# Third expert's gathers after its predecessor's weights, the fallback as one loop, and two weight splits one step later

## The chip, the core and the metric

The kernel runs on one NeuronCore of a Trainium2 chip. The time is device microseconds (us) of one execution, the median over several executions. Engines are named as in the profile: PE (TensorE, matrix multiply; PEld its weight load), DVE (VectorE), ACT (ScalarE), POOL (GpSimd), SP (SyncE, which here only issues DMAs). [...]

## The reference

Three layers in a row: a linear attention with decay, a mixture of 8 experts in which every token takes the expert of its largest logit, and a mixture of 4 experts in which every token takes all four, weighted. 3072 tokens, 256 wide, hidden width 1024, all in float32.

```python
def _moe_ref(x, w_gate, w1, w2):                # 8 experts, one per token
    logits = x @ w_gate
    expert_idx = np.argmax(logits, axis=1)
    ...
    for e in range(E):
        mask = expert_idx == e
        xe = x[mask]
        h = np.maximum(xe @ w1[e], 0.0)
        out[mask] = gate_w[mask, None] * (h @ w2[e])

def _moe2_ref(x, domain_probs, w1, w2):         # 4 experts, all of them for each token
    p = domain_probs / (domain_probs.sum(-1, keepdims=True) + 1e-09)
    for e in range(E):
        h = np.maximum(x @ w1[e], 0.0)
        out += p[:, e:e + 1] * (h @ w2[e])

def reference(**kwargs):
    x = _attn_ref(...)                           # (4, 8, 768, 32), laid out as 3072 x 256
    return _moe2_ref(x=_moe_ref(x=x, ...), ...)
```

## The kernel before, in words

Every float32 matrix product is made of three matmuls on split operands: a value is cast to a rounded high part (`hi`, on ACT) and the rest is a low part (`lo`, a subtraction on DVE or POOL); the three are hi x hi, hi x lo, lo x hi. So each weight tile has a cast and a subtraction before PE can use it.

The program has three stages on the time line of the profiled execution. From 0 to about 113 us the attention runs and each group of tokens is routed. From 113 to 288 us the eight experts of the first mixture run, in an order of turns found at run time (the fullest first). From 292 us on the second mixture runs with the order of all its instructions written out by hand.

**Experts.** For each expert `e` the loop calls `gemm1x` (eight products `f` of 6 matmuls into PSUM tile `ph`, which has 3 buffers; ACT writes `hh`, DVE writes `hl`), `make_x(e + 1)` (PE transposes the next expert's token rows `xg`, tile `tpx`) and `gemm2x` (two products of 24 matmuls into `po`). Expert 0 is done in two halves of 256 and 216 columns. `gather_turn(e)` issues up to four indirect DMAs on POOL that fetch the token rows `xg` of turn `e`; `xg` has 8 buffers. `prep` splits the next expert's weights: the subtractions of the first weight matrix (`wl`, line 152) are on POOL, those of the second (line 150) on DVE. After each product `f` a `hook` takes one entry of a list `queue`: first the computation of each expert's first slot, then that of each token's place (`pl`, `place`, `t`, `ot`, six tiles `om`, a matmul `ip`), written to DRAM as `idd`, then 24 `fetch` gathers on POOL (line 1002) which bring each token's weights for the second mixture (`pgs`). The scheduler of the language orders instructions of this stage on each engine; `issue_after` holds one back behind another.

**Fallback.** If an expert has more tokens than its columns, `tc.If(left > 0)` (line 1043) runs eight loops of plain matmuls, one for each expert. With the inputs timed here `left` is 0: the profile holds no instruction of its lines 1044 to 1083, only the branch around them. In PE's program 509 instructions of the fallback stand between the branch and the second mixture, in DVE's 243.

**Second mixture.** A step is one `hidden` (seven products of 3 matmuls each into the PSUM banks x, z, w, y, lines 1113 to 1148) and one `output` (36 matmuls into `po`, line 1174) of the step before; 64 steps, four weight pairs `i` = 0 to 3 for each of four parts of the tokens and four experts. In a step ACT copies banks x, z, w to `s`, POOL adds `g`, DVE makes `u` and `c`, ACT and DVE make the high and low parts `h`. `split_pair` casts a pair's two weight tiles on ACT (lines 178, 180) and subtracts on POOL (179, 181); `sums_pair` makes four sums on POOL (172). For the first expert pairs 0 and 1 are split before the stage; pairs 2 and 3 are split at the end of the first two steps.

Of the kernel before, what the change touches and what calls it, by code (L numbers as in the profile page):

```python
# [8 lines left out]
F32 = mybir.dt.float32  # L9
# [10 lines left out]
P = 128  # L20
# [15 lines left out]
NSL = 512  # L36
NC = E1 * NSL // P + 1
BIG = 3 << 29
OUTSIDE = 16384


def body(tc, I, out):
    nc = tc.nc
    with ExitStack() as outer:
# [5 lines left out]
        xs = dp.tile([NT, D], F32, name="xs")  # L50
        pgd = dp.tile([NT, E2], F32, name="pgd")
        idd = dp.tile([NT + P, 1], I32, name="idd")
        zero = cp.tile([P, 1], I32, name="zero")
        nc.vector.memset(zero, 0)

# [813 lines left out]
        with ExitStack() as ctx:  # L869
# [88 lines left out]
            def gather_turn(e):  # L958
                gather(e, range(tiles(e)), xs, idr.rearrange("p e c -> p (e c)"), 4 * (e - STAY))
# [52 lines left out]
            for e in range(E1):  # L1012
                if e == E1 - 2:
                    operands = x_first()

                def hook(f, e=e):
                    if operands:
                        operands.pop(0)()
                    if queue and e and (e > 1 or len(queue) > NQ):
                        queue.pop(0)()  # L1020
                    if f % 4 == 3:
                        prep(e + 1, f // 4)
                    if e == 0 and f in (4, 6):
# [12 lines left out]
                if e == 0:  # L1036
                    gemm2x(0, hs, CAP0, CAPS[0], bass.ds(BASES[0], CAPS[0] - CAP0), lambda k: prep(1, 2 + k))
                else:
                    gemm2x(e, hs, 0, CAPS[e], bass.ds(BASES[e], CAPS[e]), lambda k: prep(e + 1, 2 + k))


            left = nc.values_load(tab[0:1, 3, 0:1], min_val=0, max_val=NT)
            with tc.If(left > 0, preferred_fallthrough_block=False), tc.tile_pool(name="fall", bufs=1) as fp:
                starts = nc.values_load_multi_w_load_instructions(tab[0:1, 1, :], min_val=0, max_val=NT)[1]
                turns = nc.values_load_multi_w_load_instructions(tab[0:1, 4, :], min_val=0, max_val=E1 - 1)[1]
                ends = nc.values_load_multi_w_load_instructions(tab[0:1, 2, :], min_val=0, max_val=NT)[1]
                for e in range(E1):
                    w1, w2 = (I[k][bass.ds(turns[e], 1)].rearrange("o r c -> (o r) c") for k in ("w1", "w2"))
                    with tc.For_i(starts[e], ends[e], P) as ws:
                        ix = fp.tile([P, 1], I32, name="ixf")  # L1050
                        nc.sync.dma_start(ix, idd[bass.ds(ws, P)])
                        xg = m1.tile([P, D], F32, tag="xg", name="xgf", bufs=8)
                        nc.gpsimd.indirect_dma_start(xg, None, xs, bass.IndirectOffsetOnAxis(ap=ix, axis=0))
                        xT = m1.tile([P, 2, P], F32, tag="xg", name="xTf", bufs=8)
                        tp = pm.tile([P, 2, P], F32, tag="oneC", name="tpf", bufs=2)
                        for k in range(2):
                            nc.tensor.transpose(tp[:, k, :], xg[:, k * P:k * P + P], ident)
                        nc.scalar.copy(xT, tp)
                        hf = fp.tile([P, NF, P], F32, tag="hf", name="hf")
                        for j in range(2):  # L1060
                            raw = [mp.tile([P, 512], F32, tag="hh", name="raw0f", bufs=10) for _ in range(2)]
                            for k in range(2):
                                nc.sync.dma_start(raw[k], w1[k * P:k * P + P, j * 512:j * 512 + 512])
                            for f in range(4):
                                ph = pm.tile([P, P], F32, tag="three", name="phf", bufs=3)
                                for k in range(2):
                                    nc.tensor.matmul(ph, raw[k][:, f * P:f * P + P], xT[:, k, :],
                                                     start=(k == 0), stop=(k == 1))
                                nc.scalar.activation(hf[:, 4 * j + f, :], ph, AF.Relu)
                        raws = []  # L1070
                        for j in range(4):
                            raw = mp.tile([P, 2, D], F32, tag="hl", name="raw1f", bufs=10)
                            nc.sync.dma_start(
                                raw, w2.rearrange("(k p) d -> p k d", p=P)[:, j * 2:j * 2 + 2, :])
                            raws.append(raw)
                        for k in range(2):
                            po = pm.tile([P, P], F32, tag="two", name="pof", bufs=2)
                            for f in range(NF):
                                nc.tensor.matmul(po, raws[f // 2][:, f % 2, k * P:k * P + P], hf[:, f, :],
                                                 start=(f == 0), stop=(f == NF - 1))  # L1080
                            dst = bass.ds(ws, P)
                            (nc.vector.tensor_copy if k else nc.scalar.copy)(x2[k][:, dst], po)
                x_again()

        m1s.close()
# [125 lines left out]
        for e in range(E2):  # L1211
            g = E1 + e
            for t in range(NTP):
                tn = (t + 1) % NTP if (e, t) != (E2 - 1, NTP - 1) else None
                for i in range(4):
                    step = 4 * t + i

                    def weights(when, f):
                        for gn, at in ((g + 1, step), (g, step + 16)):
                            if E1 < gn < E1 + E2 and at in when:  # L1220
                                f(gn, when[at])

# [24 lines left out]
                    held = (*held, (i, HP)) if held else (g, t, (i, HP))  # L1247
# [37 lines left out]
```

## Time and profile before

| | |
|---|---|
| median of 3 runs | 824.31 us (822.92 to 825.62) |
| profiled execution, its own time | 822.34 us |
| its span, first to last instruction | 820.6 us |
| mean granted PE clock | 0.969 |
| PE busy | 773.1 us, 94% of the span |
| DVE, POOL, ACT busy | 580.1, 480.2, 406.2 us |

The profiled execution is 1.97 us under the median of the runs shown; 1.7 us of its time lie outside the span. An engine's busy time is a union of its instructions' times. In rows of the time line the bracket at the end is the idle time of that engine just before the row and what ended it; "issue" means that the profile shows nothing for which it waited, "remote" that a semaphore ended it whose sender was not found.

### The profile page before, as it was taken

What the parts mean: (1) busy time and instruction counts of PE and PEld (TensorE: products, weight loads), DVE (VectorE), ACT (ScalarE), POOL (GpSimd) and SP (SyncE); (2) the same over time, 40 slices, a digit from 0 to 9 for tenths busy, and PEclk for the clock granted to TensorE, in tenths of its full rate; (3) what the DMA queues carried; (4) which work ended last, traced back from release to release, by engine and by line L of the source; (5) the groups of instructions that cost most, each with busy time, mean ns of one, the idle gap of its engine ahead of it and who ended that gap; (6) DMA issues with size and microseconds to landing.
All of it is one profiled execution on the core that took longest, in us unless ns stands there. A gap on an engine that the chain in (4) does not pass through costs nothing.

```text
span 820.6 us, 16313 instructions
## 1 busy us (share of the span) xinstructions
PE 773.1 (94%) x6296; PEld 728.4 (89%) x6296; DVE 580.1 (71%) x1050; ACT 406.2 (49%) x858; POOL 480.2 (59%) x538
## 2 busy tenths in 40 slices
PE   8879987899999969999999999999999999999994
PEld 5556577789999969999999999999999999999994
DVE  8697882665445656776887777978767877778853
ACT  5533343434455445455555455565554655554540
POOL 5546645624588065356876355977435886465634
PEclk8998997999999979999999999999999999999998
DMA  8943225433843310000000000100000000000001
GB/s 220 226 124 97 64 42 178 151 109 104 122 124 118 91 30 26 2 1 27 26 27 27 1 2 1 52 27 26 2 2 1 26 27 1 1 27 28 26 27 52
DMA packets 41688, 46.41 MB, mean 57 GB/s; under 512 B 10432, under 2 KB 30656, under 8 KB 41600
## 3 DMA queue, kind: packets, MB, share of 16 engines
q1 hardware_dynamic: 37040, 37.09, 16.9%
q0 software_dynamic: 3360, 7.13, 2.9%
q8 instruction: 51, 0.84, 0.4%
q10 hardware_dynamic: 1200, 1.05, 0.4%
q14 instruction: 37, 0.30, 0.1%
HBM read 38.90 MB, written 6.35 MB: 55 GB/s over the span
## 4 chain that ended last, share of the span: by engine, by line
PE 60%; issue 1%; POOL 1%; ACT 1%; DVE 0%; POOLq 0%; ACTq 0%
PE po L1174 32%; PE x L1113 9%; PE z L1113 8%; PE w L1113 8%; PE y L1113 4%; POOL out L1194 1%; ACT s L1126 0%; ACT xc L802 0%; PE poA L1174 0%; POOLq L1281 0%; POOL g L1131 0%; ACT wh L178 0%; POOL gap L1199 0%; DVE h L1122 0%; DVE c L1148 0%
## 5 line engine op out<-in xcount | busy, mean ns | idle before, releaser
L1174 PE MATMUL po<-w,h 128*128 128x256 f32 x2280 | 281.4, 281 | 0.3 <-DVE h L1122 0.3
L1174 PEld LDWEIGHTS po<-w,h 128*128 128x128 f32 x2280 | 279.0, 189 | 0.5 <-DVE h L1122 0.5
L1119 ACT ACTIVATE h<-c 128x384 fp32r<-128x384 f32 x192 | 98.8, 525 | 150.2 <-DVE c L1148 84.8
L1122 DVE SCALAR_TENSOR_TENSOR h<-c,h 128x384 fp32r<-128x384 f32 x192 | 150.2, 791 | 11.3
L1131 POOL TENSOR_TENSOR g<-s,s 128x384 f32<-128x384 f32 x64 | 65.1, 1017 | 145.7 <-ACT s L1130 145.7
L1133 DVE TENSOR_TENSOR u<-y,s 128x384 f32<-128x384 f32 x64 | 35.5, 555 | 75.2 <-ACT s L1130 70.1
L1113 PE MATMUL x<-xc,wh 128*128 128x384 f32 x256 | 67.4, 345 | 7.5 <-issue 4.1
L803 POOL TENSOR_TENSOR xc<-x,xc 128x384 fp32r<-128x384 f32 x32 | 36.5, 1140 | 51.0 <-ACT xc L802 50.7
L1113 PE MATMUL w<-xc,wh 128*128 128x384 f32 x256 | 66.2, 340 | 0.0
L1113 PE MATMUL z<-xc,wh 128*128 128x384 f32 x256 | 66.1, 340 | 0.0
L838 ACT ACTIVATE hh<-ph 128x216 fp32r<-128x216 f32 (+8 forms) x68 | 33.5, 495 | 57.5 <-PE ph L248 38.4
L248 PE MATMUL ph<-xh,wh 128*128 128x488 f32 (+8 forms) x142 | 51.2, 361 | 10.0 <-DVE hl L840 7.7
L1148 DVE TENSOR_TENSOR c<-u,g 128x384 f32<-128x384 f32 x64 | 60.4, 944 | 0.0
L840 DVE SCALAR_TENSOR_TENSOR hl<-ph,hh 128x216 fp32r<-128x216 f32 (+8 forms) x68 | 37.5, 557 | 28.1 <-ACT hh L838 22.1
L1126 ACT COPY s<-x 128x384 f32<-128x384 f32 x64 | 30.7, 480 | 53.4 <-PE x L1113 53.4
L152 POOL TENSOR_TENSOR wl<-raw,wh 128x1024 fp32r<-128x1024 f32 (+1 forms) x22 | 39.6, 1800 | 26.8 <-ACT wh L146 25.0
L1122 DVE SCALAR_TENSOR_TENSOR h<-x,h 128x384 fp32r<-128x384 f32 x64 | 35.7, 558 | 24.8 <-ACT h L1119 24.5
L803 POOL TENSOR_TENSOR xc<-ts,xc 128x384 fp32r<-128x384 f32 x46 | 52.4, 1153 | 0.0
L1113 PEld LDWEIGHTS x<-xc,wh 128*128 128x128 f32 x256 | 42.6, 190 | 11.0 <-ACT s L1126 6.1
L501 POOL TENSOR_TENSOR Sm<-S,smask 128x256 f32<-128x256 f32 x44 | 31.3, 729 | 35.9 <-DVE S L491 29.1
L248 PE MATMUL ph<-xh,wl 128*128 128x488 f32 (+8 forms) x142 | 50.3, 354 | 0.3 <-POOL wl L152 0.3
L248 PE MATMUL ph<-xl,wh 128*128 128x488 f32 (+8 forms) x142 | 50.1, 353 | 0.0
(236 smaller groups left out, 1743.9 us busy)
## 6 DMA issues: line engine op xcount, KB each, us to landing
raw<-in_w SPq DMA_DIRECT2D x30, 512.0 KB
raw<-in_v SPq DMA_DIRECT2D x32, 256.0 KB
xs<-xo SPq DMA_DIRECT2D x24, 128.0 KB
xz<-in_xt SPq DMA_DIRECT2D x6, 384.0 KB
CT<-in_CT SPq DMA_DIRECT2D x7, 192.0 KB
BT<-in_BT SPq DMA_DIRECT2D x7, 192.0 KB
bt<-in_bt SPq DMA_DIRECT2D x3, 384.0 KB
ar<-in_ar SPq DMA_DIRECT2D x3, 384.0 KB
```

The source lines that it names most:

```text
L152: ins = nc.gpsimd.tensor_sub(lo[:, :, a:a + n], raw[:, :, a:a + n], hi[:, :, a:a + n].bitcast(F32))
L248: mm = nc.tensor.matmul(ph, w[:, k, fs], x[k], start=(i == 0), stop=(i == 5))
L803: eng.tensor_sub(o[:, 1], src, o[:, 0].bitcast(F32))
L838: i0 = nc.scalar.activation(hh, ph, AF.Relu)
L840: i1 = nc.vector.scalar_tensor_tensor(hl, ph, 0.0, hh.bitcast(F32), op0=ALU.max, op1=ALU.subtract)
L1113: nc.tensor.matmul(bank[to], w[:, a], x[:, r], start=(m == 0 and to not in seen), stop=(m == 2), skip_group_check=True)
L1119: sc.activation(HP[n][0], src, AF.Relu)
L1122: v.scalar_tensor_tensor(HP[n][1], src, 0.0, HP[n][0].bitcast(F32), op0=ALU.max, op1=ALU.subtract)
L1131: nc.gpsimd.tensor_add(g_, s5, s7)
L1133: v.tensor_add(u2, bank["y"], s1)
L1148: v.tensor_add(c22, u2, g_)
L1174: nc.tensor.matmul(two[h], x[:, ts], w2[:, w, j], start=(i, j, h * (len(hs) - 1), m) == (0, 0, 0, 0), stop=(i, j, m) == (3, 1, 2), skip_gr ...
```

## The change

Three edits.

1. In the expert stage `gather_turn(2)` moves from behind expert 0's second `gemm1x` to behind its `gemm2x`, held back until the second `wl` of expert 1 (`LOW[0]`). The hook takes entries of `queue` in every product from expert 1 on (before, only the four first ones in expert 1), so the places are computed one expert earlier, and empty entries thin the fetches to three in four products.
2. The fallback becomes one loop over a list of parts made on DVE inside the branch, and the hint that the untaken arm should follow the branch goes.
3. In the second mixture the splits of pairs 2 and 3 move from steps 0 and 1 to steps 1 and 2; the sums of pair 3 move from step 0 to step 1, behind the split of pair 2.

```diff
-            NQ = NU + NU // 4 + 6
...
-            queue += [lambda u=u: fetch(u) for u in range(NU)]
+            queue += [f for u in range(NU) for f in [lambda u=u: fetch(u)] + [lambda: None] * (u % 3 == 2)]
...
-                    if queue and e and (e > 1 or len(queue) > NQ):
+                    if queue and e:
                         queue.pop(0)()
...
-                if e + 2 < E1:
+                if 0 < e < E1 - 2:
                     gather_turn(e + 2)
...
                 if e == 0:
                     gemm2x(0, hs, CAP0, CAPS[0], bass.ds(BASES[0], CAPS[0] - CAP0), lambda k: prep(1, 2 + k))
+                    with tc.issue_after(LOW[0]):
+                        gather_turn(2)
...
-            with tc.If(left > 0, preferred_fallthrough_block=False), tc.tile_pool(name="fall", bufs=1) as fp:
-                starts = nc.values_load_multi_w_load_instructions(tab[0:1, 1, :], min_val=0, max_val=NT)[1]
...
-                for e in range(E1):
-                    w1, w2 = (I[k][bass.ds(turns[e], 1)].rearrange("o r c -> (o r) c") for k in ("w1", "w2"))
-                    with tc.For_i(starts[e], ends[e], P) as ws:
+            with tc.If(left > 0), tc.tile_pool(name="fall", bufs=1) as fp:
...
+                with tc.For_i(0, parts_, 1) as part:
+                    cell = fp.tile([1, 2], I32, name="cell")
+                    nc.sync.dma_start(cell, lid[bass.ds(part, 1)])
...
-                            if g == E1 and step < 2:
-                                if step == 0:
+                            if g == E1 and step in (1, 2):
+                                split_pair(g, step + 1)
+                                if step == 1:
                                     sums_pair(g, 3)
-                                split_pair(g, step + 2)
```

PE's order at the branch, before: the fallback's eight loops (rows of one are shown, `tpf` to `pof`) stand between the branch of line 1043 and the first product `x` of the second mixture.

```order
L859 MATMUL po<-hh,wl_7_1_3832 128x376
L1042 TENSOR_LOAD tab
L1043 COMPARE_AND_BRANCH
L1043 UNCONDITIONAL_BRANCH
L1044 TENSOR_LOAD tab
L1046 TENSOR_LOAD tab
L1049 COMPARE_AND_BRANCH
L1049 UNCONDITIONAL_BRANCH x2
```

The same place of PE's order now, whole up to the first product:

```order
L1047 COMPARE_AND_BRANCH
L1087 TENSOR_LOAD all__4053
L1088 COMPARE_AND_BRANCH
L1088 UNCONDITIONAL_BRANCH x2
L1326 BRANCH_PREFETCH_HINT
L1102 MATMUL tpf<-ident,xgf 128x128 x2
L1112 MATMUL phf<-xTf,raw0f 128x128 x16
L1124 MATMUL pof<-hf,raw1f 128x128 x16
L1088 REGISTER_ALU
L1088 COMPARE_AND_BRANCH
L1088 UNCONDITIONAL_BRANCH
L1047 UNCONDITIONAL_BRANCH x2
```

One loop stands there in place of eight: in PE's program 72 instructions now belong to the arm that is jumped over (before 509), in DVE's 69 (before 243). Before, the untaken arm stood right behind the branch and the loops after it, so the way to the second mixture crossed all of them; now the taken jump goes over the one loop.

POOL's order from the end of expert 0's first half, before. `xg` are the gathers (`idr`: the turns' rows), `wl` the weight subtractions of experts 1 and 2.

```order
L265 DMA xg<-xs,idx 128x256 x2
L265 DMA xg<-xs,idr 128x256 x8
L152 TENSOR_TENSOR wl_1_0_2423<-raw_1_0_2302,wh_1_0_2422 128x1024
L265 DMA xg<-xs,idr 128x256 x2
L152 TENSOR_TENSOR wl_1_1_2467<-raw_1_1_2304,wh_1_1_2466 128x1024
L265 DMA xg<-xs,idr 128x256 x2
L988 TENSOR_TENSOR pl<-oneh,base 128x192
L265 DMA xg<-xs,idr 128x256 x2
L152 TENSOR_TENSOR wl_2_0_2696<-raw_2_0_2693,wh_2_0_2695 128x1024
```

And now:

```order
L267 DMA xg<-xs,idx 128x256 x2
L267 DMA xg<-xs,idr 128x256 x4
L154 TENSOR_TENSOR wl_1_0_2424<-raw_1_0_2303,wh_1_0_2423 128x1024
L154 TENSOR_TENSOR wl_1_1_2468<-raw_1_1_2305,wh_1_1_2467 128x1024
L267 DMA xg<-xs,idr 128x256 x8
L990 TENSOR_TENSOR pl<-oneh,base 128x192
L267 DMA xg<-xs,idr 128x256 x2
L154 TENSOR_TENSOR wl_2_0_2697<-raw_2_0_2694,wh_2_0_2696 128x1024
```

The run of eight gathers in front of expert 1's first subtraction is now a run of four; a run of eight (those of the third and the fourth expert) stands behind its second one.

DVE's order in expert 2 (products of 456 columns), before. `ot` and `om` are operands of the places' matmul.

```order
L840 SCALAR_TENSOR_TENSOR hl<-ph,hh 128x456 x2
L227 TENSOR_SCALAR t<-place 128x24
L840 SCALAR_TENSOR_TENSOR hl<-ph,hh 128x456
L217 TENSOR_TENSOR ot<-iota_76,t 128x576
L218 TENSOR_TENSOR ot<-ot,tokc 128x576
L840 SCALAR_TENSOR_TENSOR hl<-ph,hh 128x456
L228 SCALAR_TENSOR_TENSOR m<-t,place 128x24
L840 SCALAR_TENSOR_TENSOR hl<-ph,hh 128x456
L213 TENSOR_TENSOR om<-iota_74,m 128x512
```

And now, from the first product of expert 2:

```order
L842 SCALAR_TENSOR_TENSOR hl<-ph,hh 128x456
L230 SCALAR_TENSOR_TENSOR m<-t,place 128x24
L842 SCALAR_TENSOR_TENSOR hl<-ph,hh 128x456
L215 TENSOR_TENSOR om<-iota_75,m 128x512
L842 SCALAR_TENSOR_TENSOR hl<-ph,hh 128x456
L215 TENSOR_TENSOR om<-iota_75,m 128x512
L842 SCALAR_TENSOR_TENSOR hl<-ph,hh 128x456
L215 TENSOR_TENSOR om<-iota_75,m 128x512
L842 SCALAR_TENSOR_TENSOR hl<-ph,hh 128x456
```

The two `ot` moved to the end of expert 1; one `om` now stands behind each of the second to the seventh product of expert 2, and the 24 matmuls `ip` stand behind its last product.

## Rows read from the trace of the kernel before

**Rows 1.** The page's head: busy time, share of the span, instructions.

```profile
PE 773.1 (94%) x6296; PEld 728.4 (89%) x6296; DVE 580.1 (71%) x1050; ACT 406.2 (49%) x858; POOL 480.2 (59%) x538
```

**Rows 2.** PE's waits, 105 to 330 us: total, times, longest.

```profile
PE ph L248 <- DVE hl L840: 7.7, 6, 3.0
...
PE x L1113 <- ACT s L1126: 2.6, 1, 2.6
```

**Rows 3.** The branch's line: ns min/median/max, first and last start.

```profile
L1043 PEldq COMPARE_BRANCH  x2: 95/1892/3690, 285.2 to 288.2; - x2
...
L1043 DVEq COMPARE_BRANCH  x2: 51/53/55, 288.3 to 288.7; - x2
```

**Rows 4.** Time line around the branch: start, duration, engine, line.

```profile
287.51 0.33 PE L859 MATMUL po<-hh,wl 128*128 128x376 f32 x1
...
291.90 0.56 DVE L793 TENSOR_TENSOR ts<-x,x 128x384 f32<-128x384 f32 x1 [3.47 <-issue]
...
291.96 1.01 PE L1113 MATMUL x<-xc,wh 128*128 128x384 f32 x2 [4.12 <-issue]
```

**Rows 5.** Time line of PE, ACT and POOL, steps 0 to 4 of the second mixture.

```profile
302.32 1.01 PE L1113 MATMUL x<-xc,wh 128*128 128x384 f32 x2 [2.61 <-ACT s L1126]
...
310.16 2.12 POOL L179 TENSOR_TENSOR wl<-raw,wh 128x896 fp32r<-128x896 f32 x1 [1.88 <-ACT wh L178]
311.03 0.51 PE L1113 MATMUL x<-xc,wh 128*128 128x384 f32 x2
...
314.69 4.43 PE L1174 MATMUL po<-w,h 128*128 128x256 f32 x36
...
317.88 0.52 ACT L1119 ACTIVATE h<-c 128x384 fp32r<-128x384 f32 x1 [0.71 <-DVE c L1148]
...
326.88 0.51 PE L1113 MATMUL x<-xc,wh 128*128 128x384 f32 x2
```

**Rows 6.** Stretches: length, busy of PE, PEld, DVE, ACT, POOL, granted clock.

```profile
131.00:141.20 10.20, 7.87 (x35) 7.61 (x36) 2.94 (x8) 3.69 (x9) 4.22 (x3) 0.50 0.59 195
147.00:173.00 26.00, 23.68 (x111) 19.69 (x111) 15.20 (x38) 9.82 (x15) 11.56 (x9) 1.00 0.47 151
...
291.40:294.80 3.40, 2.84 (x9) 2.84 (x10) 1.70 (x4) 1.58 (x4) 1.26 (x1) 0.50 0.03 7
301.70:308.50 6.80, 6.18 (x24) 6.18 (x25) 4.47 (x6) 2.87 (x7) 6.50 (x6) 0.50 0.28 78
```

**Rows 7.** The chain that ended last, at the turn to step 1.

```profile
300.45 0.92 ACT wh L178
...
301.89 0.38 ACT s L1126
```

**Rows 8.** Time line of POOL, ACT and PE in expert 0's second half.

```profile
123.46 0.94 POOL L265 DMA_INDIRECT xg<-xs,idr  x1 [2.03 <-DVE tab L914]
...
130.59 0.35 ACT L838 ACTIVATE hh<-ph 128x216 fp32r<-128x216 f32 x1 [5.28 <-remote]
...
131.41 0.55 PE L248 MATMUL ph<-xh,wh 128*128 128x216 f32 x1 [2.96 <-DVE hl L840]
...
132.21 0.94 POOL L265 DMA_INDIRECT xg<-xs,idr  x1 [0.30 <-issue]
...
134.94 0.55 PE L248 MATMUL ph<-xh,wh 128*128 128x216 f32 x1 [1.92 <-DVE hl L840]
```

**Rows 9.** Time line of DVE, POOL and PE in experts 1 and 2.

```profile
156.56 2.42 DVE L944 TENSOR_SCALAR nov<-nov 128x8 f32<-128x8 f32 x1
...
159.60 0.49 PE L248 MATMUL ph<-xh,wh 128*128 128x488 f32 x1 [1.92 <-DVE tab L943]
...
178.54 2.55 POOL L152 TENSOR_TENSOR wl<-raw,wh 128x1024 fp32r<-128x1024 f32 x1 [12.32 <-ACT wh L146]
...
178.89 2.82 DVE L218 TENSOR_TENSOR ot<-ot,tokc 128x576 f16<-128x576 f16 x1
...
182.31 0.48 PE L248 MATMUL ph<-xh,wh 128*128 128x456 f32 x1 [1.65 <-DVE hl L840]
```

More of the change, by code (lines that the diff above doesn't have):

```diff
@@ L38 @@
 BIG = 3 << 29
+NLIST = NU + E1
 OUTSIDE = 16384
@@ L52, in body @@
         idd = dp.tile([NT + P, 1], I32, name="idd")
+        lid = dp.tile([NLIST, 2], I32, name="lid")
         zero = cp.tile([P, 1], I32, name="zero")
@@ L1042, in body @@
             left = nc.values_load(tab[0:1, 3, 0:1], min_val=0, max_val=NT)
-            with tc.If(left > 0, preferred_fallthrough_block=False), tc.tile_pool(name="fall", bufs=1) as fp:
-                starts = nc.values_load_multi_w_load_instructions(tab[0:1, 1, :], min_val=0, max_val=NT)[1]
-                turns = nc.values_load_multi_w_load_instructions(tab[0:1, 4, :], min_val=0, max_val=E1 - 1)[1]
-                ends = nc.values_load_multi_w_load_instructions(tab[0:1, 2, :], min_val=0, max_val=NT)[1]
-                for e in range(E1):
-                    w1, w2 = (I[k][bass.ds(turns[e], 1)].rearrange("o r c -> (o r) c") for k in ("w1", "w2"))
-                    with tc.For_i(starts[e], ends[e], P) as ws:
[L1050 to L1055, printed above, removed]
-                        for k in range(2):
[L1057 to L1061, printed above, removed]
-                            for k in range(2):
[L1063 to L1082, printed above, removed]
@@ new lines, in body, with t8, wide @@
+            with tc.If(left > 0), tc.tile_pool(name="fall", bufs=1) as fp:
+                def t8(name, shape, dt=F32):
+                    return fp.tile([P, *shape], dt, name=name)
+                st, n, ni, pc, lt = t8("st", (E1,)), t8("n", (E1,)), t8("ni", (E1,), I32), t8("pc", (E1,)), t8("lt", (E1, E1))
+                v.tensor_copy(st, tab[:, 1])
+                v.tensor_copy(n, tab[:, 2])
+                v.tensor_sub(n, n, st)
+                v.tensor_scalar(n, n, 127.0, None, op0=ALU.add)
+                v.tensor_copy(ni, n)
+                v.tensor_scalar(ni, ni, 7, None, op0=ALU.logical_shift_right)
+                v.tensor_copy(n, ni)
+                v.tensor_tensor(lt, rows(nth), cols(nth), op=ALU.is_lt)
+                v.tensor_mul(lt, lt, rows(n))
+                v.tensor_reduce(pc, lt, axis=AX.X, op=ALU.add)
+                v.scalar_tensor_tensor(st, pc, -float(P), st, op0=ALU.mult, op1=ALU.add)
+                v.tensor_add(n, n, pc)
+                all_ = t8("all_", (1,), I32)
+                v.tensor_copy(all_, n[:, E1 - 1:])
+                sh = [P, NLIST, E1]
+                kk, at, ge = t8("kk", (NLIST,)), t8("at", sh[1:]), t8("ge", sh[1:])
+                lf, li = t8("lf", (NLIST, 2)), t8("li", (NLIST, 2), I32)
+                nc.gpsimd.iota(kk, pattern=[[1, NLIST]], base=0, channel_multiplier=0,
+                               allow_small_or_imprecise_dtypes=True)
+                def wide(x):
+                    return x[:, None, :].broadcast_to(sh)
+                v.tensor_tensor(at, kk[:, :, None].broadcast_to(sh), wide(pc), op=ALU.is_ge)
+                v.tensor_tensor(ge, kk[:, :, None].broadcast_to(sh), wide(n), op=ALU.is_ge)
+                v.tensor_sub(at, at, ge)
+                for i, x in enumerate((st, tab[:, 4])):
+                    v.tensor_copy(pc, x)
+                    v.tensor_mul(ge, at, wide(pc))
+                    v.tensor_reduce(lf[:, :, i:i + 1].rearrange("p k o -> p (k o)"), ge, axis=AX.X, op=ALU.add)
+                v.scalar_tensor_tensor(lf[:, :, 0:1].rearrange("p k o -> p (k o)"), kk, float(P),
+                                       lf[:, :, 0:1].rearrange("p k o -> p (k o)"), op0=ALU.mult, op1=ALU.add)
+                v.tensor_copy(li, lf)
+                nc.sync.dma_start(lid.rearrange("k c -> (k c)")[None], li[0:1].rearrange("p k c -> p (k c)"))
+                parts_ = nc.values_load(all_[0:1, 0:1], min_val=0, max_val=NLIST)
+                with tc.For_i(0, parts_, 1) as part:
+                    cell = fp.tile([1, 2], I32, name="cell")
+                    nc.sync.dma_start(cell, lid[bass.ds(part, 1)])
+                    ws = nc.values_load(cell[0:1, 0:1], engines=(mybir.EngineType.SP, mybir.EngineType.Activation,
+                                                                 mybir.EngineType.DVE), min_val=0, max_val=NT)
+                    turn = nc.values_load(cell[0:1, 1:2], engines=(mybir.EngineType.SP,), min_val=0, max_val=E1 - 1)
+                    w1, w2 = (I[k][bass.ds(turn, 1)].rearrange("o r c -> (o r) c") for k in ("w1", "w2"))
+                    ix = fp.tile([P, 1], I32, name="ixf")
+                    nc.sync.dma_start(ix, idd[bass.ds(ws, P)])
+                    xg = m1.tile([P, D], F32, tag="xg", name="xgf", bufs=8)
+                    nc.gpsimd.indirect_dma_start(xg, None, xs, bass.IndirectOffsetOnAxis(ap=ix, axis=0))
+                    xT = m1.tile([P, 2, P], F32, tag="xg", name="xTf", bufs=8)
+                    tp = pm.tile([P, 2, P], F32, tag="oneC", name="tpf", bufs=2)
+                    for k in range(2):
+                        nc.tensor.transpose(tp[:, k, :], xg[:, k * P:k * P + P], ident)
+                    nc.scalar.copy(xT, tp)
+                    hf = [mp.tile([P, 4, P], F32, tag="hl", name="hf", bufs=10) for _ in range(2)]
+                    for j in range(2):
+                        raw = [mp.tile([P, 512], F32, tag="hh", name="raw0f", bufs=10) for _ in range(2)]
+                        for k in range(2):
+                            nc.sync.dma_start(raw[k], w1[k * P:k * P + P, j * 512:j * 512 + 512])
+                        for f in range(4):
+                            ph = pm.tile([P, P], F32, tag="three", name="phf", bufs=3)
+                            for k in range(2):
+                                nc.tensor.matmul(ph, raw[k][:, f * P:f * P + P], xT[:, k, :],
+                                                 start=(k == 0), stop=(k == 1))
+                            nc.scalar.activation(hf[j][:, f, :], ph, AF.Relu)
+                    raws = []
+                    for j in range(4):
+                        raw = mp.tile([P, 2, D], F32, tag="hl", name="raw1f", bufs=10)
+                        nc.sync.dma_start(
+                            raw, w2.rearrange("(k p) d -> p k d", p=P)[:, j * 2:j * 2 + 2, :])
+                        raws.append(raw)
+                    for k in range(2):
+                        po = pm.tile([P, P], F32, tag="two", name="pof", bufs=2)
+                        for f in range(NF):
+                            nc.tensor.matmul(po, raws[f // 2][:, f % 2, k * P:k * P + P], hf[f // 4][:, f % 4, :],
+                                             start=(f == 0), stop=(f == NF - 1))
+                        dst = bass.ds(ws, P)
+                        (nc.vector.tensor_copy if k else nc.scalar.copy)(x2[k][:, dst], po)
```

## Prediction

> **What bounds the kernel now.** I read the page's head first: PE is busy 94% of the span [rows 1], so only time in which PE waits, or runs at the lower clock, can be won. The list of PE's waits between 105 and 330 us, the stretch that the edits touch, comes second: `ph` waits for DVE's `hl` 7.7 us in six pieces, the longest 3.0, and a product `x` waits once 2.6 us for ACT's `s` [rows 2]. The branch's own line comes third: of PE's two branch instructions one took 95 ns, the other 3690 ns; DVE's took some 53 ns each [rows 3]. The time line shows what follows: PE's last product of the first mixture starts at 287.51 and ends, by the spacing of the rows, at 287.84, and the first `x` of the second mixture starts at 291.96, after 4.12 us of "issue"; DVE stands 3.47 us although its branch was over at 288.7 [rows 4]. No engine was waited for there. [...]
>
> **The branch and the second mixture.** From 287.84 to the start of step 4 at 326.88 are 39.04 us. The two steps from 311.03 to 326.88 have no wait: 15.85 us, 7.92 a step [rows 5]; of that the output is 4.27 (`po` begins at 314.69, one step after 311.03 the next product would begin at 318.95), the seven products 3.66. Four sets of products and three outputs lie before step 4: 4 x 3.66 + 3 x 4.27 = 27.45. The other 11.6 us are loss: 4.12 at the branch, 2.61 for `s`, and about 4.5 of half clock (half of PE's 2.84 and 6.18 busy us in the two low stretches [rows 6]), the rest in small waits of 0.2 or less.
>
> The branch. The new order has one loop to jump over, and the taken jump of PE passes 72 instructions, not 509. PE's short branch instruction costs 95 ns, DVE's 53 ns [rows 3]; I take that PE's taken one will be of that size, so that `x` starts at about 288.6, when DVE has evacuated the last `po` and passed its own branch (288.7). That leaves 0.75 of the 4.12. Both ends: 3.7 stays (the branch costs what the row shows), or 0.1 stays. The profile does not show a short taken jump on PE; I take the value of the nearest short ones.
>
> [...]
>
> The start. Without the pause, the products meet the operands that DVE, ACT and POOL make from 288.7 on, one after the other. Placing the durations of the old rows in the new order gives three short waits, together 1.3 us, before PE reaches product 4 of step 0.
>
> Step 0 to 1. Before, two casts of pair 2 stood on ACT before step 1's `s` (300.45 to 301.89) [rows 7], and product 4 of step 1 waited 2.61 for it [rows 5]. They go. ACT's next obstacle is step 0's last `h`, which needs `c`, which needs POOL's `g`: `s` stands behind it in ACT's order. The casts are 1.44 of the 2.61 us; with them away about 1.2 stay, and 0.25 more come as PE arrives earlier relative to DVE: 1.45.
>
> Steps 1 to 3. Now pair 2 is cast at the end of step 1 and used at the start of step 2, pair 3 a step later. In step 2 before, the last `h` begins at 317.88, 3.2 us after the output's begin; cast 0.92 [rows 7] after its end (318.3), then POOL's `wl` 2.12 [rows 5]: 318.3 + 0.85 + 2.1 = 321.3, while the third matmul of the next product would be due at 318.95 + 0.35 = 319.3. That is a wait of 2.0 us, twice (the end of step 1 has two fewer casts on ACT in front of that `h`, which makes the first some 0.3 shorter): 1.7 + 2.0 = 3.7. The split was hidden before, since a whole step lay between it and its use; this cover goes. The ends are 2.6 (both `h` a half us earlier) and 4.6. These waits stand between the 1.92 that left the clock at 1.00 and the 2.61 that did not, so I take full clock, with half clock as a rival.
>
> Sum of this part: 0.75 + 27.45 + 1.3 + 1.45 + 3.7 + 0.3 for small waits = 34.95 against 39.04: 4.1 us less. The edits thus work against each other: branch and clock give about 8, the later splits take back nearly 4.
>
> **Gathers and places.** Before, eight gathers stand on POOL from 123.46 to 133.15, 1.25 us apart. In the same stretch ACT starts `hh` 5.28 us after its last work, released by "remote", and PE waits 2.96 and 1.92 for `hl` [rows 8]; 10.2 us at half clock follow, with PE 7.87 busy [rows 6], about 3 of them loss. That the gathers cause the late releases is only a coincidence in time. After, four gathers stand there and eight behind the second `wl` of expert 1, beside expert 1's first products of 488 columns. Ends: all 4.88 + 3 = 7.9 us are won, or the same two waits come to expert 1, whose work in the 10.2 us would be slowed as well, about 10 lost. Since the same number of gathers runs either way, I take 1.0 gained, near nothing.
>
> Two waits come from DVE: `nov`, only 8 elements, lasts 2.42 us at 156.56, and `ot` 2.82 us at 178.89 beside POOL's `wl` of 2.55; PE then waits 1.92 and 1.65 [rows 9]. After, `ot` stands at the end of expert 1, away from that `wl`, while expert 2's DVE has one `om` behind each of six products. I count 1.65 won. For `nov` the `wl` beside it comes behind two more gathers, so it may pass or may not: half, 0.95. Ends of both together: 3.6 won, or 3.6 lost again at other places. The 24 matmuls `ip` move but do not change. The indices are written one expert earlier, and empty entries thin the fetches: 0, since POOL has idle time there (12.32 us ahead of one `wl` [rows 9]); were that cover gone, a late `wl` would cost about a wait as above, 1.9. The list-making of the new fallback is not executed when the branch is taken: 0.
>
> **Sum.** 4.1 + 1.0 + 1.65 + 0.95 = 7.7. The profiled execution took 822.34: 814.6 in the same manner; it lies 1.97 under the median of the runs shown, and from that median, 824.31, the forecast is 816.6.
>
> **The rivals.** *The branch still pays.* The taken jump may cost PE 3.7 us whatever its length: nothing in the profile shows a short one. Then 291.4 to 294.8 stays low, and of the 4.1 some 1.0 is left (the 2.61 shrinks, the later splits wait instead): 819.7. The equal case is that the branch is cheap and the two 2-us waits lower the clock as 2.61 did, some 3 us: 819.6. *The gathers were the cause in expert 0.* Speaking for it, the late releases end as the run ends; against it, the profile names no link between a gather and the release. All 7.9 are won and nothing comes back: 816.6 - 6.9 = 809.7. *Slower: the run of eight falls on expert 1.* POOL issues eight in a row in front of expert 1's products, the releases come late there, two waits of 4.9 us together and half clock through 10 us of work, 5 more, while the first place keeps its own waits (had they come from the stage and not from the gathers): the 1.0 is not won and 10 are lost, 827.6. It decides from the point where it exceeds the 6.7 of the other terms. *The change does not do what it says:* waits go from one place to the next, and 823 to 825 remain.
>
> **How the numbers follow.** About 0.3% (2.5 us) can be told from no change, so 821.8 and 826.8 are the bounds. Forecast 816.6, own range 813 to 820 (the ends of the second mixture, 2.6 to 4.6, and of DVE's waits): 0.50. Branch or clock still pays, 819.7: 0.19. Gathers fully won, 809.7: 0.13. Nothing, 824: 0.09. Slower, 827.6: 0.09. Faster: 0.50 + 0.13 + 0.16 of the second case = 0.79; same 0.13; slower 0.08. The range takes in the gathers' gain and cuts off the slower case: 809.5 to 823.5.
>
> **What would show it.** Right: PE's idle time between the last `po` of the first mixture and the first `x` under 1 us, granted clock 1.00 after it, waits of 1.5 to 2 us for `wl` at steps 2 and 3, no wait for `ot` in expert 2, step 4 about 35 us after the end of the first mixture. Wrong: a PE branch of microseconds, low clock in steps 1 to 3, late releases of `ph` in expert 1, or PE waits of 3 us in expert 0 gone altogether.

## The result, and the profile after

| | median, runs | range |
|---|---|---|
| before, same chip | 825.62 us, 19 | 820.78 to 828.43 |
| after | 815.34 us, 19 | 810.47 to 821.65 |

The ratio is 0.9885, 95% interval 0.9868 to 0.9902: 10.3 us between the medians, 9.5 by the ratio. The forecast was 816.6, a ratio of 0.9907. On two other chips the same kernel had 0.9940 (0.9915 to 0.9964) and 0.9886 (0.9852 to 0.9920); the kernel before had 818.6 and 825.8 there.

The changed kernel's profiled execution took 816.07 us, 814.4 of it span, 6.2 less than the span before. That one pair understates the change, since much of its time is chance (below). The list of PE's waits from 105 to 330 us (total, times, longest) answers to [rows 2]; ahead of the arrow is what PE was to do, behind it what it waited for:

```profile
PE ph L250 <- DVE hl L842: 5.0, 4, 2.3
PE x L1158 <- POOL wl L181: 3.2, 2, 1.7
PE ip L225 <- DVE om L215: 3.1, 4, 2.0
PE x L1158 <- ACT s L1171: 1.5, 2, 1.3
PE po L861 <- DVE hl L842: 1.4, 1, 1.4
...
PE x L1158 <- PEq L1047: 0.3, 1, 0.3
```

The 4.1 us of "issue" have become 0.3 of PE's own queue, the wait for `s` fell from 2.6 to 1.3, and two waits for `wl`, 3.2 us together, are new. New in the experts are a wait of 1.4 us for `hl` in front of a product `po` and two more waits of `ip` for `om`; the wait of 1.92 behind `nov` [rows 9] is gone. The branch's line, which answers to [rows 3], has no long instruction left:

```profile
L1047 PEldq COMPARE_BRANCH  x1: 228/228/228, 281.5 to 281.5; - x1
...
L1047 DVEq COMPARE_BRANCH  x1: 72/72/72, 284.6 to 284.6; - x1
```

The time line at the turn, which answers to [rows 4]: the last product of the first mixture, DVE's evacuation, the first product of the second mixture.

```profile
283.82 0.33 PE L861 MATMUL po<-hh,wl 128*128 128x376 f32 x1
284.19 0.55 DVE L866 COPY x<-po 128x376 f32 x1 [3.01 <-PE po L861]
...
284.45 0.89 PE L1158 MATMUL x<-xc,wh 128*128 128x384 f32 x2 [0.30 <-PEq L1047]
```

PE starts 0.63 us after its last start, where before it took 4.45. The stretches behind it (columns as in [rows 6]) are steps 0 and 1, step 2, step 3:

```profile
284.40:300.10 15.70, 13.47 (x78) 11.51 (x78) 12.07 (x21) 8.53 (x19) 7.42 (x7) 1.00 0.01 2
300.10:310.30 10.20, 8.48 (x57) 7.95 (x57) 5.30 (x8) 5.58 (x13) 8.32 (x9) 1.00 0.21 53
310.30:320.30 10.00, 8.24 (x57) 7.92 (x58) 4.94 (x9) 5.33 (x13) 7.70 (x6) 1.00 0.19 52
```

The clock is 1.00 throughout, where [rows 6] had two stretches at 0.50. But steps 2 and 3 take 10.2 and 10.0 us, where a step without a wait took 7.92. The time line at the start of step 2 shows why: ACT's cast of pair 2, POOL's subtraction behind it, and PE's third matmul of the first product waiting for it.

```profile
299.19 0.93 ACT L180 CAST wh<-raw 128x896 fp32r<-128x896 f32 x1
...
300.18 0.62 PE L1158 MATMUL x<-xc,wh 128*128 128x384 f32 x2
300.20 2.08 POOL L181 TENSOR_TENSOR wl<-raw,wh 128x896 fp32r<-128x896 f32 x1 [2.35 <-ACT wh L180]
...
302.33 0.44 PE L1158 MATMUL x<-xc,wl 128*128 128x384 f32 x1 [1.54 <-POOL wl L181]
```

Lengths between starts of PE's products, read from the time lines, in us (the last two columns are further executions, described below):

| stretch | before | after | after_again | no_s_beside |
|---|---|---|---|---|
| start to expert 0 | 113.1 | 110.7 | 114.9 | 113.9 |
| expert 0 | 33.9 | 31.4 | 26.8 | 30.6 |
| expert 1 | 24.9 | 24.7 | 23.0 | 24.5 |
| experts 2 and 3 | 42.9 | 46.1 | 42.1 | 42.1 |
| experts 4 to 6 | 56.4 | 54.5 | 54.5 | 54.5 |
| last `po` to first `x` | 4.1 | 0.3 | 0.3 | 0.4 |
| step 0 to step 4 | 34.9 | 35.9 | 37.2 | 32.9 |
| step 4 to the end | 493.7 | 494.0 | 494.1 | 494.2 |

The first row has the same instructions in all four and varies by 4 us. Expert 0 varies by 5 us in the changed kernel (28.4 in *after_beside*), and by 7 us over *before*, *f_alone* and *s_alone*, which have the same order there. What belongs to the change must be read from stretches that repeat, and from medians.

### The profile page after: what moved, and what is told of

It reads as the page before. It is cut to its first block, busy times and chain, and to the rows that moved or that the text cites. A ratio compares the mean times of both kernels' runs of the same rounds, so it can differ in the third digit from the quotient of the medians.

```text
span 814.4 us, 16308 instructions
## 1 busy us (share of the span) xinstructions
PE 772.7 (95%) x6296; PEld 725.7 (89%) x6296; DVE 580.6 (71%) x1050; ACT 405.6 (50%) x858; POOL 478.5 (59%) x538
## 4 chain that ended last, share of the span: by engine, by line
PE 58%; POOL 3%; issue 1%; ACT 1%; DVE 0%; POOLq 0%; ACTq 0%; DVEq 0%
PE po L1219 31%; PE x L1158 8%; PE z L1158 8%; PE w L1158 7%; PE y L1158 4%; POOL out L1239 1%; POOL wl L181 1%; ACT s L1171 0%; POOL g L1176 0%; ACT xc L804 0%; POOL xc L805 0%; POOL ts L795 0%; PE poA L1219 0%; POOL raw L174 0%; POOL w L183 0%
## 5 line engine op out<-in xcount | busy, mean ns | idle before, releaser
L1167 DVE SCALAR_TENSOR_TENSOR h<-c,h 128x384 fp32r<-128x384 f32 x192 | 149.4, 787 | 11.5
L1171 ACT COPY s<-x 128x384 f32<-128x384 f32 x64 | 30.6, 478 | 56.2 <-PE x L1158 56.2
L861 PE MATMUL po<-hl,wh 128*128 128x488 f32 (+8 forms) x142 | 48.1, 339 | 1.4 <-DVE hl L842 1.4
```

The lines of the kernel that those rows point to most:

```text
L861: mm = nc.tensor.matmul(po, w[:, f % 4, ks], h, start=(i == 0), stop=(i == 23))
L1167: v.scalar_tensor_tensor(HP[n][1], src, 0.0, HP[n][0].bitcast(F32), op0=ALU.max, op1=ALU.subtract)
```

## The experiments

The kernels of one group ran on one chip with the kernel before beside them.

**First group: each part alone, and all but the split move.** Before had 819.71 us here. The edits are the diff's own parts.

*f_alone*, the fallback alone:

```diff
-            with tc.If(left > 0, preferred_fallthrough_block=False), tc.tile_pool(name="fall", bufs=1) as fp:
+            with tc.If(left > 0), tc.tile_pool(name="fall", bufs=1) as fp:
...
-                for e in range(E1):
+                with tc.For_i(0, parts_, 1) as part:
```

> The kernel before with the fallback edit alone (one loop, no hint on the order of the arms). Theory A (the long taken jump costs PE 3.7 us and sets off the half clock that follows): PE's idle time between the two mixtures falls from 4.1 to about 0.3 us, step 0 runs at granted clock 1.00, the wait for ACT's s at step 1 stays near 2.6 to 2.9 us since the two casts still stand before it; 5 to 6 us faster if the clock holds after that wait, about 3 if it falls to 0.50 as before. Rival B (the pause is only hidden time, operands of step 0 are late anyway): the same waits appear as waits for DVE and ACT, under 1.5 us faster.

Ratio 0.9973 (0.9954 to 0.9991), about 2.2 us. PE's waits, 276 to 332 us:

```profile
PE x L1156 <- ACT s L1169: 3.2, 2, 2.9
...
PE x L1156 <- PEq L1045: 0.3, 1, 0.3
```

The pause goes (theory A), step 0 runs at 1.00, the wait for `s` grows to 2.9, and part of the half clock stays behind it: step 0 to step 4 takes 34.4 us, as in *no_s* below (34.5), where the clock was 0.54 for 3.5 us behind the same wait, and not 32.9 as in *no_s_beside*, where it held 1.00. So it is the "about 3" of A's two cases. In the profile the way from the last `po` to step 4 takes 34.7 us against 39.0, more than the 2.2 that the whole kernel won.

*g_alone*, the gathers and the list:

```diff
-                if e + 2 < E1:
+                if 0 < e < E1 - 2:
                     gather_turn(e + 2)
...
+                    with tc.issue_after(LOW[0]):
+                        gather_turn(2)
```

> The kernel before with the moved gathers and the earlier list of places and fetches alone. Theory A (the run of eight gathers on POOL makes PE's semaphores late): the waits of 2.96 and 1.92 us in expert 0 go, expert 1 gets some back, the waits for nov and ot mostly go: about 4 us faster. Rival B (late releases follow the writes of 3072 pieces of 16 and 4 bytes to DRAM, pgd near 114 us and idd near 200 us, by some ten us, whatever gathers run): a wait in expert 0 stays in some form, and the one after the idd write moves with that write from expert 4 to expert 3, where it costs 2 to 3 us: 1 to 3 us faster.

Ratio 0.9946 (0.9920 to 0.9972), about 4.4 us, the size that A gave. But its first ground fell: in this profile expert 0 has four gathers in front and still a wait of 2.9 us for `hl`, while f_alone and s_alone, with eight, pass expert 0 in 26.6 and 27.3 us against 33.9 in the profile before. Nor did the wait for `nov` go: 1.8 us of it stay, and expert 1 takes 26.5 us against 24.9. What repeats is later: experts 2 and 3 take 42.1 us and experts 4 to 6 take 54.5, as in the changed kernel, so these two gains come from this part. No late release (work of DVE or ACT that starts microseconds after the product of PE it needs) stands in expert 3 here, so B's price did not show.

*s_alone*, the splits:

```diff
-                            if g == E1 and step < 2:
-                                if step == 0:
+                            if g == E1 and step in (1, 2):
+                                split_pair(g, step + 1)
+                                if step == 1:
                                     sums_pair(g, 3)
-                                split_pair(g, step + 2)
```

> The kernel before with the two splits moved one step later, alone. Theory A (a wait of 1.5 to 1.7 us for wl at steps 2 and 3 is the price, the end of the wait for s at step 1 the gain): the 4.1 us pause and the half clock right after it stay, the wait for s falls from 2.6 to about 1.3 us, the half clock behind it goes (some 3 us), two new waits for wl of 3.2 us together: between 2 us faster and 1 us slower. Rival B (the splits were hidden in their old place, and the low clock there came from the pause at the branch alone): 3 us slower.

Ratio 1.0032 (1.0011 to 1.0052): 2.6 us slower, close to B's 3. The pause of 3.9 us stays, two waits for `wl` of 3.2 together come; the wait for `s` falls to 0.9, but step 0 to step 4 takes 38.0 us against 34.9. A's gain came (step 1 runs at 1.00 and takes 6.2 us for 8.7); its price was too low, since steps 2 and 3 take 10.2 and 11.5 us for 7.9 each, the last partly below full clock (0.85). B's ground does not hold: in *no_s*, without the pause, the clock was still 0.54 from 289.0 to 292.5 us, behind the wait of 2.9 us for `s`.

*no_s*, the changed kernel with the splits in their old place (the diff above, reversed).

> The changed kernel with the two splits back in steps 0 and 1. Theory A: no wait for wl at steps 2 and 3 (3.2 us), a wait of 2.6 to 2.9 us for s at step 1 in place of 1.3; about 1.5 to 2 us faster than the changed kernel if the clock stays at 1.00, about 1 to 2 us slower if it falls to 0.50 behind that wait. Rival B (the later splits are free): equal or slower by the whole wait, with the clock at 1.00.

809.03 us, ratio 0.9884 (0.9862 to 0.9907). Step 0 to step 4 takes 34.5 us. By the ratio that is 9.5 us, where f_alone and g_alone, its two parts, add up to 6.6; the intervals are too wide to tell these apart. Since the changed kernel ran on another chip, the comparison was made again in the third group.

**Second group.** Before had 818.64 us here.

*after_again*, the changed kernel.

> The changed kernel once more, beside the others of this call on one chip. Both theories: 1.0 to 1.3% faster than the kernel before; it is the measure for the other three. Its waits in expert 0's second half differ from those of the first profile by a us or more if they are chance, and repeat (1.70 and 0.36 us) if the order of the gathers sets them.

812.50 us, ratio 0.9940 (0.9915 to 0.9964): 0.6% faster, where 1.0 to 1.3 was expected. Expert 0 shows one wait of 1.7 us and no late release, expert 3 none. The waits are thus chance in part. This execution lost clock behind the first wait for `wl` (0.65 over 3.5 us, 0.92 over the next 6.1), where the profile after stayed at 1.00 (stretches during that wait and after it):

```profile
294.00:296.00 2.00, 0.62 (x3) 0.30 (x2) 0.00 (x0) 0.56 (x2) 1.88 (x1) 1.00 0.00 0
296.00:299.50 3.50, 3.25 (x12) 3.25 (x13) 0.24 (x1) 1.45 (x3) 3.42 (x7) 0.65 0.48 138
299.50:305.60 6.10, 6.10 (x44) 5.97 (x43) 5.11 (x8) 3.65 (x8) 2.98 (x3) 0.92 0.03 9
```

The same wait costs 1.3 us more when the clock falls behind it (37.2 for 35.9).

*idd_pgd*, without the two writes of 3072 tiny pieces. Late releases had come behind both: in the profile before `pgd` is issued at 114.5 us and ACT starts late at 130.59, `idd` at 200.8 and ACT at 214.03 (after 6.8 us of "remote"); in the profile after `pgd` at 112.2 and ACT at 127.98, `idd` at 179.5 and DVE at 193.10.

```diff
-                nc.sync.dma_start(pgd.rearrange("(u p) e -> p u e", p=P), prob)
+                nc.sync.dma_start(pgd.rearrange("(p u) e -> p u e", p=P), prob)
...
-                nc.sync.dma_start(idd[:NT].rearrange("(u p) o -> p (u o)", p=P), idc)
...
             with tc.If(left > 0), tc.tile_pool(name="fall", bufs=1) as fp:
+                nc.sync.dma_start(idd[:NT].rearrange("(u p) o -> p (u o)", p=P), idc)
```

> The changed kernel with the two writes of 3072 tiny pieces taken out of the way: pgd is written with 384 contiguous bytes for each partition (the fetches' indices follow), and idd is written inside the fallback, which alone reads it. Theory A (PE's semaphores come late because of these tiny pieces): no late release in expert 0's second half and none in expert 3 (DVE's and ACT's first work there starts within 0.3 us after PE's), no half clock there; 3 to 7 us faster than the changed kernel, and less spread. Rival B (late releases come with the gathers on POOL): the waits stay, under 1 us of difference.

811.77 us, ratio 0.9925 (0.9898 to 0.9952): not to be told from the changed kernel beside it. Theory A's price is refuted; expert 0's wait of 1.9 us is still there. ACT's time line in expert 0 shows whose it is:

```profile
131.92 0.35 ACT L842 ACTIVATE hh<-ph 128x216 fp32r<-128x216 f32 x1 [0.31 <-PE ph L252]
133.99 1.04 ACT L150 CAST wh<-raw 128x1024 fp32r<-128x1024 f32 x1 [1.72 <-DMA raw<-in_w]
...
134.94 0.82 ACT L842 ACTIVATE hh<-ph 128x216 fp32r<-128x216 f32 x3
```

The cast of expert 1's weights waits 1.72 us for their load, and three `hh` stand behind it in ACT's order; PE waits for what they feed. This wait stands in the profiles of the changed kernel as well (1.45 us at 131.57, 1.57 at 132.87). It is read, not tested.

*idd_pgd_no_s*, the same with the splits back in steps 0 and 1.

> The kernel of the run before with the two splits back in steps 0 and 1. Theory A (the later splits cost 3.2 us of waits for wl and win 1.3 to 1.6 us of the wait for s): 1.0 to 2.0 us faster than the same kernel with the later splits, with one stretch of half clock of 3.4 us or none after the wait of 2.9 for s. Rival B (behind a wait of 2.9 us the clock always falls to 0.50 and takes back what is won): no difference of over 0.5 us.

807.61 us, ratio 0.9892 (0.9847 to 0.9936), 4.2 us under idd_pgd by medians, 2.7 by the ratios, with one of six executions at 817.2; step 0 to step 4 takes 34.5 us against 35.9. A's direction, more than its size; the intervals overlap.

*hint*, the changed kernel with the old order of the two arms:

```diff
-            with tc.If(left > 0), tc.tile_pool(name="fall", bufs=1) as fp:
+            with tc.If(left > 0, preferred_fallthrough_block=False), tc.tile_pool(name="fall", bufs=1) as fp:
```

> The changed kernel with the old hint, so that the untaken arm stands right behind the branch and PE crosses the one loop by a jump at the arm's end. Theory A (what cost 3.7 us was the distance of the jump, 509 instructions): PE's pause between the mixtures stays at 0.3 to 0.5 us, same time as the changed kernel. Rival B (the order of the arms set it): the pause is 4 us again and some of the half clock behind it, 3 to 6 us slower.

811.61 us, ratio 0.9923 (0.9902 to 0.9945), like after_again. PE crosses by two branch instructions as in [rows 3], and neither is long; the pause is 0.6 us:

```profile
L1047 PEldq COMPARE_BRANCH  x2: 90/138/185, 275.6 to 278.5; - x2
...
L1047 DVEq COMPARE_BRANCH  x2: 51/53/55, 278.6 to 279.0; - x2
```

So the amount of program to be crossed set the 3.7 us, not the order of the arms. The DMAs in the trace show what moved in the pause. From 288 to 292 us in the kernel before, four packets move, 0.04 MB, all of the kind `instruction`:

```profile
q8 instruction: 1, 0.02, 2.0%
q14 instruction: 3, 0.02, 1.8%
```

The pauses of g_alone and s_alone, which keep the eight loops, hold the same four; in those of the changed kernel, f_alone and hint no packet of that kind moves. So packets of that kind move in the pause behind the long branch of 3690 ns, and none behind the short ones of 185 and 228 ns. They are not bound to a pause: two more move from 292 to 293 us in the kernel before, where PE works again. That these DMAs set the length of the pause is read from this coincidence and not tested by itself, and only these two lengths of program, 509 and 72 instructions, were run.

**Third group.** Before had 825.79 us here.

*after_beside*, the changed kernel.

> The changed kernel as the measure for the other three on one chip. Both theories: 0.5 to 1.3% faster than the kernel before; step 0's start to step 4's start 35.9 to 37.3 us, with two waits for wl of 1.5 and 1.7 us.

817.61 us, ratio 0.9886 (0.9852 to 0.9920). Its six times fall into two heaps, 810.1 to 810.4 and 817.4 to 818.7.

*no_s_beside*, the splits in steps 0 and 1.

> The changed kernel with the splits of pairs 2 and 3 back in steps 0 and 1, beside the changed kernel. Theory A (the later splits are a net loss once the pause is gone): step 0 to step 4 takes 34.5 us, 1.4 to 2.8 less, and the whole is 2 to 4 us faster than the changed kernel. Rival B (the chips differ, the splits are free): within 1 us of it.

811.42 us, ratio 0.9824 (0.9791 to 0.9858): 6.2 us under the changed kernel by medians, 5.1 by the ratios; the ends of the two intervals just meet. PE's waits, 276 to 335 us:

```profile
PE x L1158 <- ACT s L1171: 3.1, 2, 2.9
PE x L1158 <- PEq L1047: 0.4, 1, 0.4
```

No wait for `wl` is left. This execution held 1.00 behind the wait of 2.9 (step 0 to step 4 in 32.9 us); no_s fell to 0.54 there (34.5). A's direction again, and B's "within 1 us" does not fit the medians. But the size leans on the two heaps: the two profiled executions, 810.13 and 811.59 us, lie the other way round, since expert 0 and expert 1 were longer in this one.

*s_mid*, both splits in step 1, behind its copies `s`:

```diff
                         if n in (1, 3):
                             store_out()
+                        if g == E1 and step == 1 and n < 2:
+                            split_pair(g, n + 2)
...
-                            if g == E1 and step in (1, 2):
-                                split_pair(g, step + 1)
-                                if step == 1:
-                                    sums_pair(g, 3)
+                            if g == E1 and step == 0:
+                                sums_pair(g, 3)
```

> The changed kernel with both splits in step 1, each cast behind that step's three copies s (pair 2 in front of the first h, pair 3 behind it), the sums of pair 3 in step 0 again. Theory A (what costs is where the casts stand in ACT's order: ahead of s they hold up step 1, at the end of a step they hold up the next one's third matmul): the wait for s falls to about 1.3 us, no wait for wl, no half clock; step 0 to step 4 takes about 33 us, 1 to 2 us less than with the splits in steps 0 and 1. Rival B (POOL or ACT has no room in step 1): new waits for h of 1 us and more, no gain.

811.72 us, ratio 0.9827 (0.9800 to 0.9853). ACT's time line in step 1 has the casts behind `s`:

```profile
291.20 0.46 ACT L1171 COPY s<-x 128x384 f32<-128x384 f32 x1
291.56 0.48 ACT L1173 COPY s<-z 128x384 f32<-128x384 f32 x1
291.93 0.49 ACT L1175 COPY s<-w 128x384 f32<-128x384 f32 x1
292.30 0.96 ACT L180 CAST wh<-raw 128x896 fp32r<-128x896 f32 x1
...
293.66 0.51 ACT L1164 ACTIVATE h<-x 128x384 fp32r<-128x384 f32 x1
294.04 0.96 ACT L180 CAST wh<-raw 128x896 fp32r<-128x896 f32 x1
```

PE's waits for `s` are 1.8 us in two, none for `wl`, and step 0 to step 4 takes 31.6 us at full clock, the shortest of all: theory A in this stretch, 1.3 under no_s_beside, which also held the clock. In the whole time it equals no_s_beside; a gain of 1 to 2 us cannot be told there. Both beat before and after.

*unthinned*, the fetches without empty entries:

```diff
-            queue += [f for u in range(NU) for f in [lambda u=u: fetch(u)] + [lambda: None] * (u % 3 == 2)]
+            queue += [lambda u=u: fetch(u) for u in range(NU)]
```

> The changed kernel with a fetch in every product again, without the empty entries. Theory A (three fetches in place of four in front of each wl are what makes experts 3 to 6 shorter by 0.85, 0.8, 0.6 and 0.5 us): PE waits for POOL's wl come back in experts 4 to 6, some 0.5 us each; 1.5 to 2.5 us slower than the changed kernel. Rival B (the earlier list and not its density does it): same time.

818.04 us, ratio 0.9897 (0.9857 to 0.9938), like the changed kernel. Its one PE wait from 185 to 278 us is the 2.4 us for `hl` behind a late release in expert 3; none for `wl` comes back, and experts 4 to 6 take 54.9 us (54.5 thinned, 56.4 before). Theory A fell: B, the list begun one expert earlier, fits. All eleven profiles with the earlier list have 54.3 to 55.0 us for these three experts, the three with the old one 56.4 to 57.7.

## Why the prediction was right, point by point

**The branch** was priced at 0.75 us left of 4.12; 0.30 is left, and `hint` shows that the amount of program to be crossed was the cause and not the order of the arms. That half clock right after it would go held: step 0 ran at 1.00 in the profiles after, after_again, f_alone and s_mid, each with the short jump.

**The second mixture to step 4** was put at 34.95 us from the last `po`, 4.1 less; it measured 36.2, 2.8 less, and 37.5 where the clock fell. Steps 0 and 1 took 15.7 us, where two sets of products and one output without waits give 11.6: 4.1 lost, 3.05 forecast. In this the wait for `s` was right (1.27 with 0.24 before it, 1.45 forecast). The mis-sized term is "1.3 for the start and 0.3 for small waits": 2.6 in place of 1.6. In step 2 the third matmul comes 2.15 us after the first one, 1.8 beyond the 0.35 it takes without a wait, and in step 3 it is 2.0, as forecast (3.7 for both); but the two steps took 20.2 us for 15.85, so 4.35 are lost, the rest in small pieces. With 0.45 better at the branch, 1.1 worse in steps 0 and 1 and 0.65 worse in steps 2 and 3, these are the 1.3 us between 36.2 and 34.95. The other miss is the clock: it was taken as full behind the 2-us waits, with half clock a rival (in the profile before it was 0.50 behind waits of 2.96, 4.12 and 2.61 us, and 1.00 around one of 1.92). With waits for `wl` of up to 1.7 us both happened, in different executions: 1.00 in the profile after, 0.65 over 3.5 us in after_again, where it cost 1.3 us, not the 3 of the rival.

**The later splits** were the part forecast as working against the rest, by nearly 4. That stands in direction: alone 2.6 us slower, and with the short jump 4.2 and 6.2 us by the medians of the two pairs that ran side by side, 2.7 and 5.1 by the ratios. The stretch to step 4 explains 1.4 to 4.3 of it in the profiled executions; whether more belongs to it is open.

**Gathers, 1.0.** The step "only a coincidence in time" was right. With eight or with four gathers in front, expert 0 took 26.6 to 33.9 and 26.6 to 31.4 us. The part is worth nothing that shows there; the rivals with 7.9 won or 10 lost did not come. One sign that was to show the prediction wrong did come, PE waits of 3 us in expert 0 gone altogether. It says nothing, since they are gone in f_alone and s_alone as well, with eight gathers in front.

**`nov`, 0.95, and `ot`, 1.65.** The long DVE work beside POOL's `wl` stays (2.65 and 2.55 us in the profile after). Whether PE waits for it differs between executions. In the profile after it does, in front of a product `po` that needs the `hl` queued behind the long `nov`:

```profile
157.72 2.55 DVE L954 TENSOR_TENSOR nov<-nov,by 128x8 f32<-128x8 f32 x1
...
160.98 0.49 PE L861 MATMUL po<-hl,wh 128*128 128x488 f32 x1 [1.43 <-DVE hl L842]
```

Of the eleven profiles with the moved gathers and the earlier list, seven have expert 1 in 23.0 to 23.1 us, so all of `nov`'s wait is won; three (after, no_s_beside, s_mid) have this wait of 1.4 in its place and 24.5 to 24.7 us; in g_alone the old wait stays. The 0.95 was the mean of two cases that both occur. In expert 2 the wait for `ot` is gone. The 24 matmuls `ip` that moved in cost the same 0.8 us as before in expert 3, but they now wait 0.9 us for `om` (PE's waits of `ip`, before from 105 to 330 us, and after in expert 2 alone):

```profile
PE ip L223 <- DVE om L213: 2.2, 2, 2.0
PE ip L225 <- DVE om L215: 0.9, 2, 0.5
```

So experts 2 and 3 together win 0.8, half of the 1.65, where no late release falls into expert 3.

**The earlier list, 0.** This step failed: "0, since POOL has idle time there" was argued from one `wl`, far from the fetches. Experts 4 to 6 are 1.9 us shorter, repeatedly, and g_alone shows that it comes from this part. Before, POOL was late there for `wl` and DVE for `hl` (waits of PE's products and of its weight loads, PEld, 214 to 271 us):

```profile
PE ph L248 <- DVE hl L840: 0.8, 2, 0.6
PE ph L248 <- POOL wl L152: 0.3, 1, 0.3
PEld ph L248 <- DVE hl L840: 1.5, 2, 1.0
PEld ph L248 <- POOL wl L152: 0.6, 1, 0.6
```

In the profile after these experts have no such wait.

**The sum.** For after_again against before, without expert 0 and the start, it is 1.9 (expert 1) + 0.8 + 1.9 + 3.8 and 2.3 lost in the second mixture, 6.1 us. Expert 1's part and the clock's 1.3 in it change from execution to execution. The medians give 6.1 us on that chip and 8 to 10 on the others; that 6.1 stands twice is chance, since the profile before was taken on another chip than after_again. The total came out near 7.7 because a gain left out stood against a loss that was too small, and that is luck: of the forecast's parts only the branch and the waits for `s` and for `wl` came out near their size. What the medians show beyond these stretches, 2 to 4 us, is not explained.

## What to carry to other kernels

Code that is never executed can cost: here PE stood 4.1 us at the jump over 509 instructions of it and 0.3 at the one over 72 (0.6 with the old order of the arms). The profile shows it as "issue" behind a branch instruction of 3690 ns, with four packets of the kind `instruction` in the pause. Before work is put later in an engine's order, ask what stands behind it there: casts ahead of the next step's copies came with a wait of 2.9 us for `s` (no_s_beside), casts at a step's end with two for `wl` in the steps behind, 3.2 us together, and casts just behind the copies with none for `wl` and 1.8 us for `s` (s_mid). Where a kernel's executions spread by 1%, compare stretches over several profiles first, since one profile's wait may be chance.

## What was not expected of the hardware

By the profile, DVE and ACT sometimes start microseconds after the work of PE that they need. In expert 3 of the profile after, the last matmul of `po` ended at 189.65; DVE's copy of it and ACT's first `hh` started here:

```profile
193.10 0.63 DVE L866 COPY x<-po 128x456 f32 x1 [5.60 <-PE ph L250]
...
193.18 1.36 ACT L840 ACTIVATE hh<-ph 128x424 fp32r<-128x424 f32 x3 [5.14 <-PE ph L250]
```

That is some 3.4 us after the end of that `po`, while PE's own next products went on until 193.13; the rows name one of those products as the releaser, so what held the two back is not read from them. PE then waited 2.30 us and ran at 0.50 from 195.4 to 198.4. Of the nine profiles with the moved list and the tiny writes, two had this in expert 3 (PE's waits of 2.3 us here and 2.4 in unthinned), of the two without the writes none: too few to name a cause, and it stays open. It is one source of the spread between executions of one kernel: experts 2 and 3 took 46.1 us here and 42.1 in after_again.
